# Fused windowed attention and two-layer SiLU network on one core: tile 0's first layer takes a whole batch of 576 tokens, and the zeros of the opening's constants move from GpSimd to VectorE

## The chip, the cores and the metric

The kernel runs on one core of a Trainium2 chip. The metric is the device time of one execution in microseconds (us). All executions quoted here were in the fast state of the chip; their mean granted TensorE clock was 0.988 to 1.000. Engines: PE is TensorE (PEld its weight loads), DVE is VectorE, ACT is ScalarE, POOL is GpSimd, SP is SyncE. All clock times of a trace count from the start of its span, which is some 1.8 us shorter than the device time (301.1 against 302.87 us).

## The reference

Causal attention over a window of 64 positions, then a network of two layers on its output:

```python
B, H, S, D = 8, 8, 576, 64                       # q, k, v: float32
scores = q @ k.T / sqrt(D)                       # kept where 0 <= pos_q - pos_k < 64
attn   = softmax(scores) ; o = attn @ v
x = o.transpose(0, 2, 1, 3).reshape(4608, 512)   # 8 batches x 576 tokens
h = x @ w_in                                     # 512 -> 2048
g = h * sigmoid(h)                               # SiLU
out = g @ w_out                                  # 2048 -> 512, float32
```

## The kernel before

The program is put in order when it is built: each operation joins a queue of its class with a modelled duration, and a list scheduler emits one instruction stream per engine by rank. Four points matter here.

GpSimd issues nearly all loads (these convert float32 to bfloat16 on the way) and also makes the constants. Its stream at the start is four q/k loads, the identity, the window mask, two more q/k loads, four v loads, ten w_in loads, then the rows of batch 1 mixed with eight pieces of w_out.

```python
FIRST, SPLIT, SECOND_LOADS = 6, 12, "0w1w2w3vwvwvwvww"
...
def const_ident(_):
    nc.gpsimd.memset(ident, 0.0)
    nc.gpsimd.affine_select(out=ident, in_=ident, compare_op=ALU.not_equal, fill=1.0, ...)

def const_window(_):
    nc.gpsimd.memset(window, 0.0)
    nc.gpsimd.affine_select(out=window, ...)       # twice
...
def load_w_in(a, lo, hi):
    nc.gpsimd.dma_start(out=w_in_sb[:, 2 * a:2 * a + 2, lo:hi], in_=w_in[256 * a:256 * a + 256, lo:hi]...)
```

PE is kept warm by filler matmuls on `ident` until the exponentials of batch 0 are out:

```python
def warm(op):
    nc.tensor.matmul(banks[op["bank"][0]][:, 0:384], lhsT=ident, rhs=ident..., start=True, stop=True)
p.add_filler(60, "warm", {"PE": 0.26}, warm, [c_ident], gate=lambda: exps[0][-1]["seen"] is None, pool="all")
```

The network works on nine tiles of 512 tokens: first layer (16 output blocks, 4 matmuls each), SiLU into a `g` buffer per block, second layer. Attention comes out in groups of 192 tokens through `bridge`, the transposed attention output that the first layer reads, so tile 0 takes 6 blocks in two parts, and tile 1 takes 12:

```python
work = [(ft, 0, TT) for ft in range(NFT)]                 # TT = 512, NFT = 16
if j == 0:
    work = [(ft, lo, hi) for lo, hi in ((0, 192), (192, TT)) for ft in range(FIRST)] + work[FIRST:]
elif j == 1:
    work = [(ft, lo, hi) for lo, hi in ((0, 256), (256, TT)) for ft in range(SPLIT)] + work[SPLIT:]
```

Tile 0's second layer goes piece by piece through w_out, because w_out is still landing: each of the eight pieces serves eight of its 64 matmuls. The attention of the next batch is interleaved in the second layers.

```python
order = [(m, f, 0, d_model) for m in range(4) for f in range(NFT)]
if j == 0:
    order = [(m, f, 0, d_model) for f in range(NFT) for m in range(4)]
```

The softmax here doesn't subtract the row's maximum and nothing guards it: scores larger than these inputs give would overflow.

Of the kernel before, what the change touches and what calls it, by code (L numbers as in the profile page):

```python
# [9 lines left out]
BF16 = mybir.dt.bfloat16  # L10
# [4 lines left out]
class Plan:  # L15
# [31 lines left out]
    def run(self):  # L47
# [4 lines left out]
        table, left = "exp", self.count  # L52
        pipe, sent = {True: 1.8, False: 0.0}, []
        events, order = [0.0], []
# [68 lines left out]
def kernel(ctx, tc, q, k, v, w_in, w_out, out):  # L123
    nc = tc.nc
# [12 lines left out]
    NN, NNB, NE, NOT, NGT = 8, 8, 12, 4, NFT + 3  # L137
    FIRST, SPLIT, SECOND_LOADS = 6, 12, "0w1w2w3vwvwvwvww"
    FIRST_LOADS = [(x[0], int(x[1])) for x in "q0 k0 q1 k1 q2 q3 k2 k3 v0 v1 v2 v3".split()]
# [11 lines left out]
    ident = keep.tile([128, 128], BF16, name="ident")  # L151
    zero = keep.tile([128, NP], FP32, name="zero")
    spare = keep.tile([128, NP], FP32, name="spare")
    window = keep.tile([128, 64], BF16, name="window")
# [11 lines left out]
    oxs = [keep.tile([128, 3, 2, D], BF16, name=f"ox{i}") for i in range(NOX)]  # L166
    gts = [keep.tile([128, TT], BF16, name=f"g{i}") for i in range(NGT)]
    ots = [keep.tile([128, d_model], FP32, name=f"ot{i}") for i in range(NOT)]
# [7 lines left out]
        {"at": range(4), "pv": range(4, 6), "mp": range(4, 8), "all": range(8)},  # L176
        rank=dict(prime=-8, early=-10, one=-9, first=-9, dma=-1, ld0=-1, st=-2, silu=-3, out=-2, pv=0, s=1, moe=99, warm=200, turn=2,
                  norm=0, inverse=0, bridge=0, exp=1, mask=1, lift=2, block=2, shift=2, cast=4, late=5, clear=9),
        rank0=dict(turn=-6, cast=-6, lift=-5, shift=-4.5, exp=-4, mask=-4, inverse=-3.5, norm=-3, bridge=-3.2),
# [6 lines left out]
    def const_ident(_):  # L186
        nc.gpsimd.memset(ident, 0.0)
        nc.gpsimd.affine_select(out=ident, in_=ident, compare_op=ALU.not_equal, fill=1.0,
                                base=0, channel_multiplier=1, pattern=[[-1, 128]])

    def const_window(_):

        nc.gpsimd.memset(window, 0.0)
        nc.gpsimd.affine_select(out=window, in_=window, compare_op=ALU.is_ge, fill=-32768.0,
                                base=-1, channel_multiplier=1, pattern=[[-1, 64]])
        nc.gpsimd.affine_select(out=window, in_=window, compare_op=ALU.is_ge, fill=-32768.0,
                                base=64, channel_multiplier=-1, pattern=[[1, 64]])
# [17 lines left out]

    c_ident = p.add("one", {"POOL": 1.3}, const_ident)
    c_vv = [p.add("one", {"DVE": 0.25}, lambda _, i=i: clear_vv(i)) for i in range(NV)]
    c_k = [p.add("one", {"DVE": 0.15}, lambda _, i=i: clear_k(i)) for i in range(NK)]
    c_zero = p.add("one", {"DVE": 0.1}, lambda _: nc.vector.memset(zero, 0.0))
    c_window = p.add("one", {"POOL": 0.6}, const_window)  # L220
    c_bias = [p.add("one", {"DVE": 0.9}, const_bias, [c_window])]
# [6 lines left out]
    def load_first_cast(w, u, kk):  # L228
        nc.gpsimd.dma_start(out=natbs[w][:, 0:S], in_=two(u, kk))  # L229
# [106 lines left out]
    def expo(bank, n):  # L336
        nc.scalar.activation(out=es[n % NE], in_=at_six(bank), func=ACTF.Exp, scale=scale)  # L337
# [30 lines left out]
    def first_layer(bank, j, ft, c, lo, hi):  # L368
        nc.tensor.matmul(  # L369
            banks[bank["bank"][0]][:, lo:hi], lhsT=w_in_sb[:, c, ft * 128:(ft + 1) * 128],  # L370
            rhs=bridge[:, (j * TT + lo) // 64:(j * TT + hi) // 64, c], start=(c == 0), stop=(c == NDC - 1),
        )

    def silu(bank, gt, lo, hi):
        nc.scalar.activation(out=gts[gt][:, lo:hi], in_=banks[bank["bank"][0]][:, lo:hi], func=ACTF.Silu)  # L375

# [34 lines left out]
    def add_first_batch():  # L411
        got = {}
        for what, u in FIRST_LOADS:
# [6 lines left out]
            if u == 0:  # L420
                i = n_nat[0] % NN
                n_nat[0] += 1
                ld = p.add("ld0", {"SP": 0.45}, lambda _, i=i, kk=kk: load_first(i, kk), dma=-0.15 if kk == 0 else 0.7)
                ca = p.add("cast", {"ACT": 0.7, "DVE": 0.56}, lambda e, i=i, w=w: cast_first(e, i, w), [ld])
                nat_free[i] = [ca]
            else:
                ca = p.add("early" if (what, u) in FIRST_LOADS[2:6] else "dma", {"POOL": 0.6}, lambda _, w=w, u=u, kk=kk: load_first_cast(w, u, kk), dma=0.8)
            got[what, u] = (w, ca)
# [33 lines left out]
    def add_v_loads(b, parts, busy):  # L462
        v_landed.setdefault(b, []).extend(
            p.add("dma", {"POOL": 1.0}, lambda e, part=part: load_v(e, b, part), busy, dma=1.1, lat=MARGIN * (b > 0)) for part in parts)

    def add_batch_v(b):
        busy = pv_last.get(b - NV, []) + [c_vv[b % NV]]
        if b >= NIV:
            add_v_loads(b, range(NP), busy)
        lv = v_landed[b]  # L470
        for a, z in ([(i, i + 1) for i in range(NP)] if b < NK else [(0, NP)]):
            sh = [p.add("shift", {"DVE": 0.34, "ACT": 0.64} if b == 0 else {"DVE": 0.1 + 0.18 * (z - a)}, lambda e, hf=hf, a=a, z=z: shift_v(e, b, hf, a, z),
                        lv[a:z], b=b) for hf in range(2)]
            for pj in range(a, z):
                v_done[(b, pj // 2)] = v_done.get((b, pj // 2), []) + sh + [lv[pj]]
# [7 lines left out]
    def add_unit(b, g, which, n0):  # L483
# [11 lines left out]
        for i in range(2 * na):  # L495
            ex = p.add("exp" + first, {"ACT": 0.5}, lambda _, i=i: expo(s["bank"][i], 2 * n0 + i), [s], table="exp", b=b)
            s["untils"][i].append(ex)
            exps.setdefault(b, []).append(ex)
            if b:
                ex = p.add("mask", {"DVE": 0.37}, lambda _, i=i: masking(2 * n0 + i, g), [ex, *c_mask], b=b)  # L500
            ready.append(ex)
# [22 lines left out]
    n_ot, free_ot = [0], {}  # L524

    def add_tile(j):
        gt = {}
        for ft in range(NFT):
            gt[ft] = (n_gt[0] % NGT, [])
            n_gt[0] += 1  # L530
        work = [(ft, 0, TT) for ft in range(NFT)]
        if j == 0:
            work = [(ft, lo, hi) for lo, hi in ((0, 192), (192, TT)) for ft in range(FIRST)] + work[FIRST:]
        elif j == 1:
            work = [(ft, lo, hi) for lo, hi in ((0, 256), (256, TT)) for ft in range(SPLIT)] + work[SPLIT:]
        for i, (ft, lo, hi) in enumerate(work):
# [36 lines left out]
        free_gt.update(uses)  # L573

    add_first_batch()
    add_batch_v(0)


    def warm(op):
        nc.tensor.matmul(banks[op["bank"][0]][:, 0:384], lhsT=ident, rhs=ident.unsqueeze(1).to_broadcast([128, 3, 128]),  # L580
                         start=True, stop=True)

    p.add_filler(60, "warm", {"PE": 0.26}, warm, [c_ident], gate=lambda: exps[0][-1]["seen"] is None,
                 pool="all")
# [52 lines left out]
```

## Time and profile before

| | us |
|---|---|
| device time, median of 3 (range) | 302.37 (302.01 to 303.3) |
| span of the profiled execution | 301.1 |
| last landing of w_in / of w_out piece 5 (pieces counted from 0) | 26.25 / 46.30 |
| start of tile 0's second layer / its last matmul's end | 34.15 / 52.86 |
| start of tile 1's second layer | 69.79 |

The prediction below reads most views of this profile. One that it only summarises also belongs here: the timeline of GpSimd before 27 us. Columns: start, length, engine, line, operation, output<-input, how many in a row, and in brackets the idle time before it and what ended that.

```profile
5.93 4.00 POOL L253 DMA_DIRECT2D vv<-in_v_dram  x4
9.89 7.12 POOL L259 DMA_DIRECT2D w_in_sb<-in_moe_w_in_dram  x10
...
26.53 1.20 POOL L239 DMA_DIRECT2D nat<-in_k_dram  x2 [1.01 <-DMA w_in_sb<-in_moe_w_in_dram]
```

The reader sees an engine that does nothing but issue. A v load holds it 1.00 us, a w_in load 0.71 us, a load of rows 0.60 us. From 4.80 to 17 us it has no gap. Then its later issues wait, one by one, for w_in landings: in this trace it never has more than eight loads of its own in flight. The third row load of k waits for the last w_in landing (26.25 us) and comes 0.28 us after it. From there GpSimd issues again without a gap until the w_out piece at 38.48, the one that lands at 46.30.

### The profile page before, as it was taken

What the parts mean: (1) busy time and instruction counts of PE and PEld (TensorE: products, weight loads), DVE (VectorE), ACT (ScalarE), POOL (GpSimd) and SP (SyncE); (2) the same over time, 40 slices, a digit from 0 to 9 for tenths busy, and PEclk for the clock granted to TensorE, in tenths of its full rate; (3) what the DMA queues carried; (4) which work ended last, traced back from release to release, by engine and by line L of the source; (5) the groups of instructions that cost most, each with busy time, mean ns of one, the idle gap of its engine ahead of it and who ended that gap; (6) DMA issues with size and microseconds to landing.
All of it is one profiled execution on the core that took longest, in us unless ns stands there. A gap on an engine that the chain in (4) does not pass through costs nothing.

```text
span 301.1 us, 8386 instructions
## 1 busy us (share of the span) xinstructions
PE 290.4 (96%) x3588; PEld 145.0 (48%) x3588; DVE 138.0 (46%) x330; ACT 173.1 (57%) x319; POOL 118.0 (39%) x177
## 2 busy tenths in 40 slices
PE   4989988999999999999999999999999999999996
PEld 2555444674544454445444544445444544444444
DVE  2591377977885379436950694066005520000000
ACT  4686453786456754774477438663767366226511
POOL 8957986959797989870400000000000000000000
DMA  8999999999999999991580110011101100010012
GB/s 169 166 171 174 158 164 171 225 130 110 188 169 132 108 182 170 164 105 72 65 86 2 51 59 35 3 37 72 37 0 36 73 37 0 35 72 36 0 70 73
DMA packets 82982, 28.64 MB, mean 95 GB/s; under 512 B 72448, under 2 KB 78208, under 8 KB 82944
## 3 DMA queue, kind: packets, MB, share of 16 engines
q0 software_dynamic: 77184, 18.07, 65.0%
q1 hardware_dynamic: 5760, 10.03, 9.3%
q8 instruction: 28, 0.46, 0.7%
q14 instruction: 10, 0.08, 0.1%
HBM read 36.70 MB, written 9.44 MB: 153 GB/s over the span
## 4 chain that ended last, share of the span: by engine, by line
PE 82%; POOL 9%; DMA 6%; issue 1%; DVE 1%; ACT 1%; POOLq 0%; ACTq 0%; DVEq 0%
PE mp L378 39%; PE mp L369 37%; DMA w_in_sb<-in_moe_w_in_dram 3%; PE mp L349 3%; PE at L331 3%; DMA w_out_sb<-in_moe_w_out_dram 3%; POOL vv L253 2%; POOL w_in_sb L259 2%; POOL nat L239 2%; POOL natb L229 1%; POOL w_out_sb L265 1%; ACT g L375 0%; DVE ot L384 0%; PE at L349 0%; DVE qt L246 0%
## 5 line engine op out<-in xcount | busy, mean ns | idle before, releaser
L378 PE MATMUL mp<-w_out_sb,g 128*128 128x512 bf16 (+2 forms) x608 | 130.2, 368 | 1.8 <-DMA w_out_sb<-in_moe_w_out_dram 1.8
L369 PE MATMUL mp<-bridge,w_in_sb 128*128 128x512 bf16 (+3 forms) x648 | 129.0, 355 | 1.7 <-DVE bridge L363 0.7
L375 ACT ACTIVATE g<-mp 128x512 bf16<-128x512 f32 (+3 forms) x162 | 87.6, 550 | 34.1 <-PE mp L369 32.3
L369 PEld LDWEIGHTS <-w_in_sb 128*128 128x128 bf16 x648 | 62.3, 97 | 66.2 <-issue 8.2
L378 PEld LDWEIGHTS <-g 128*128 128x128 bf16 x608 | 56.1, 98 | 63.5 <-issue 2.7
L384 ACT COPY ot<-mp 128x512 f32<-128x512 f32 (+2 forms) x36 | 20.2, 563 | 59.9 <-PE mp L378 46.1
L340 DVE TENSOR_TENSOR e<-e,mask 128x384 bf16<-128x384 bf16 x84 | 25.9, 347 | 50.0 <-ACT e L337 49.5
L337 ACT ACTIVATE e<-at 128x384 bf16<-128x384 f32 x90 | 37.2, 495 | 19.6 <-PE at L331 19.4
L239 POOL DMA_DIRECT2D nat<-in_k_dram x56 | 34.1, 617 | 13.7 <-DMA vv<-in_v_dram 5.8
L253 POOL DMA_DIRECT2D vv<-in_v_dram x32 | 32.2, 1020 | 13.4 <-PE mp L349 13.4
L239 POOL DMA_DIRECT2D nat<-in_q_dram x56 | 35.2, 649 | 2.9 <-DMA w_in_sb<-in_moe_w_in_dram 1.9
L363 DVE STREAM_TRANSPOSE bridge<-ox 128x384 bf16<-128x384 bf16 x48 | 24.8, 552 | 0.0
L246 DVE STREAM_TRANSPOSE qt<-nat 128x576 bf16<-128x576 bf16 x28 | 20.7, 786 | 6.8 <-DMA nat<-in_q_dram 6.8
L246 DVE STREAM_TRANSPOSE kt<-nat 128x576 bf16<-128x576 bf16 x28 | 20.6, 781 | 4.3 <-DMA nat<-in_k_dram 4.3
L359 DVE TENSOR_TENSOR ox<-mp,rc 128x384 bf16<-128x384 f32 x43 | 21.4, 535 | 0.1
L356 DVE RECIPROCAL rc<-mp 128x6 f32<-128x6 f32 x43 | 8.0, 190 | 19.7 <-PE mp L349 19.0
L349 PEld LDWEIGHTS <-e 128*32 128x32 bf16 x1152 | 10.9, 95 | 9.4 <-issue 7.9
L299 DVE COPY vv<-vv 64x576 bf16<-64x576 bf16 (+1 forms) x14 | 7.9, 567 | 13.9 <-DMA vv<-in_v_dram 7.7
L349 PE MATMUL mp<-vv,e 128*32 128x65 bf16 x1032 | 12.2, 194 | 0.0
L337 ACT ACT_TABLE_LOAD x7 | 9.0, 1283 | 5.4 <-PE at L331 5.3
L331 PE MATMUL at<-qt,kt 32*128 32x64 bf16 x1008 | 11.5, 190 | 0.0
L331 PEld LDWEIGHTS <-kt 32*128 32x128 bf16 x1008 | 9.3, 92 | 4.3 <-issue 3.4
(50 smaller groups left out, 79.4 us busy)
## 6 DMA issues: line engine op xcount, KB each, us to landing
out_dram<-ot SPq DMA_DIRECT2D x35, 256.0 KB, 2.4
vv<-in_v_dram POOLq DMA_DIRECT2D x32, 144.0 KB, 5.9
nat<-in_q_dram POOLq DMA_DIRECT2D x56, 72.0 KB, 4.5
nat<-in_k_dram POOLq DMA_DIRECT2D x56, 72.0 KB, 3.9
w_out_sb<-in_moe_w_out_dram POOLq DMA_DIRECT2D x8, 256.0 KB, 6.3
w_in_sb<-in_moe_w_in_dram POOLq DMA_DIRECT2D x6, 256.0 KB, 8.4
w_in_sb<-in_moe_w_in_dram POOLq DMA_DIRECT2D x4, 128.0 KB, 4.9
natb<-in_q_dram POOLq DMA_DIRECT2D x3, 144.0 KB, 4.9
```

Source lines behind the costliest of these rows:

```text
L239: nc.gpsimd.dma_start(out=nats[i][32 * h:32 * h + 32].rearrange("p (m x) -> p m x", m=NB), in_=(q, k)[kk][b, 4 * a + h].rearrange("(m p r) ...
L246: nc.vector.transpose(out=to[:, (2 * a + part) * S:(2 * a + part + 1) * S].rearrange("x (m t r) -> x m r t", t=32, r=2), in_=nats[i].rearr ...
L253: queue[e].dma_start(out=vv[b % NV][:, 2 * g0 + 1:2 * g1 + 1:2, 0:D], in_=v[b].rearrange("h s d -> (h s) d").rearrange("(g p) d -> p g d", ...
L331: nc.tensor.matmul(at_six(op["bank"][h])[:, a, x], lhsT=kt[b % NK][r, at:at + 128], rhs=qt[b % NK][r, at:at + 64], start=(s == a == x == 0 ...
L337: nc.scalar.activation(out=es[n % NE], in_=at_six(bank), func=ACTF.Exp, scale=scale)
L340: nc.vector.tensor_mul(es[n % NE], es[n % NE], mask0 if g == 0 else mask)
L349: nc.tensor.matmul(at_pv(bank)[32 * h:32 * h + 32, x, t], lhsT=e_of(b, a, n, h)[:, x, 32 * t:32 * t + 32], rhs=vv[b % NV][:, (4 * a + h) * ...
L359: nc.vector.tensor_mul(oxs[n % NOX], at_pv(bank)[:, :, :, 0:D], rcs[n % NRC].unsqueeze(3).to_broadcast([128, 3, 2, D]))
L363: nc.vector.transpose(out=bridge[:, n0:n0 + 3, 2 * a:2 * a + 2].rearrange("x t s (u i) -> x t s u i", u=2), in_=oxs[n % NOX].rearrange("p ...
L369: nc.tensor.matmul(banks[bank["bank"][0]][:, lo:hi], lhsT=w_in_sb[:, c, ft * 128:(ft + 1) * 128], rhs=bridge[:, (j * TT + lo) // 64:(j * T ...
L375: nc.scalar.activation(out=gts[gt][:, lo:hi], in_=banks[bank["bank"][0]][:, lo:hi], func=ACTF.Silu)
L378: nc.tensor.matmul(banks[bank["bank"][0]][:, 0:hi - lo], lhsT=gts[gt][:, m * 128:(m + 1) * 128], rhs=w_out_sb[:, f, lo:hi], start=(f == 0) ...
```

## The change

The intent is to use the time before 60 us better. Tile 0's first layer takes all 576 tokens of batch 0 while it waits for w_out anyway, so that tile 1 needs only 448; 64 columns of each SiLU block are then copied to tile 1's buffer. The zeros of the constants go to VectorE, the last two q/k loads are issued before the window mask, and the fillers run on a tile of zeros from the first microsecond. One w_out piece moves back in the load order, and some numbers of the scheduler's model are replaced by measured ones.

```diff
-        pipe, sent = {True: 1.8, False: 0.0}, []
+        pipe, sent = {True: 2.0, False: 0.0}, []
-    FIRST, SPLIT, SECOND_LOADS = 6, 12, "0w1w2w3vwvwvwvww"
+    FIRST, SPLIT, SECOND_LOADS = 8, 14, "0w12ww3vwvwvwvww"
+    blank = keep.tile([128, 128], BF16, name="blank")
-    gts = [keep.tile([128, TT], BF16, name=f"g{i}") for i in range(NGT)]
+    gts = [keep.tile([128, NB * 64], BF16, name=f"g{i}") for i in range(NGT)]
@@ ranks: new classes edge=-8.5 (window mask), dma0=-8.7 (last two q/k loads), rest=3 (copies)
     def const_ident(_):
-        nc.gpsimd.memset(ident, 0.0)
     def const_window(_):
-        nc.gpsimd.memset(window, 0.0)
-    c_ident = p.add("one", {"POOL": 1.3}, const_ident)
+    c_zeros = [p.add("one", {"DVE": 0.1}, lambda _, t=t: nc.vector.memset(t, 0.0)) for t in (blank, ident, window)]
+    c_ident = p.add("one", {"POOL": 0.3}, const_ident, c_zeros)
-    c_window = p.add("one", {"POOL": 0.6}, const_window)
+    c_window = p.add("edge", {"POOL": 0.5}, const_window, c_zeros)
+    def rest_of_first(e, g0, g1):
+        copies[e](out=gts[g1][:, 0:NB * 64 - TT], in_=gts[g0][:, TT:NB * 64])
@@ first_layer and silu: the bank is used from column 0
-                ca = p.add("early" if (what, u) in FIRST_LOADS[2:6] else "dma", ..., dma=0.8)
+                ca = p.add("early" if (what, u) in FIRST_LOADS[2:6] else "dma0", ..., dma=0.74)
@@ v loads of batch 0 1.1 -> 1.0, exponentials 0.5 -> 0.39 + 0.2 latency, ScalarE only for later shifts
         if j == 0:
-            work = [(ft, lo, hi) for lo, hi in ((0, 192), (192, TT)) for ft in range(FIRST)] + work[FIRST:]
+            work = [(ft, lo, hi) for lo, hi in ((0, 192), (192, NB * 64)) for ft in range(FIRST)]
+            work += [(ft, lo, hi) for ft in range(FIRST, NFT) for lo, hi in ((0, 256), (256, NB * 64))]
         elif j == 1:
-            work = [(ft, lo, hi) for lo, hi in ((0, 256), (256, TT)) for ft in range(SPLIT)] + work[SPLIT:]
+            done = NB * 64 - TT
+            work = [(ft, lo, hi) for lo, hi in ((done, 256), (256, TT)) for ft in range(SPLIT)]
+            work += [(ft, done, TT) for ft in range(SPLIT, NFT)]
+            for ft in range(NFT):
+                g0, si = gt_first[0][ft]
+                cp = p.add("rest", {"DVE": 0.12, "ACT": 0.24}, lambda e, ...: rest_of_first(e, g0, g1), ...)
@@ fillers
-        nc.tensor.matmul(banks[...][:, 0:384], lhsT=ident, rhs=ident..., start=True, stop=True)
+        nc.tensor.matmul(banks[...][:, 0:384], lhsT=blank, rhs=blank..., start=True, stop=True)
-    p.add_filler(60, "warm", {"PE": 0.26}, warm, [c_ident], ...)
+    p.add_filler(60, "warm", {"PE": 0.26}, warm, c_zeros, ...)
```

More of the change, by code (lines that the diff above doesn't have):

```diff
@@ L176 @@
         {"at": range(4), "pv": range(4, 6), "mp": range(4, 8), "all": range(8)},
-        rank=dict(prime=-8, early=-10, one=-9, first=-9, dma=-1, ld0=-1, st=-2, silu=-3, out=-2, pv=0, s=1, moe=99, warm=200, turn=2,
-                  norm=0, inverse=0, bridge=0, exp=1, mask=1, lift=2, block=2, shift=2, cast=4, late=5, clear=9),
+        rank=dict(prime=-8, early=-10, one=-9, edge=-8.5, first=-9, dma=-1, ld0=-1, dma0=-8.7, st=-2, silu=-3, out=-2, pv=0, s=1, moe=99, warm=200, turn=2,
+                  norm=0, inverse=0, bridge=0, exp=1, mask=1, lift=2, block=2, shift=2, cast=4, rest=3, late=5, clear=9),
         rank0=dict(turn=-6, cast=-6, lift=-5, shift=-4.5, exp=-4, mask=-4, inverse=-3.5, norm=-3, bridge=-3.2),
@@ L369, in first_layer @@
         nc.tensor.matmul(
-            banks[bank["bank"][0]][:, lo:hi], lhsT=w_in_sb[:, c, ft * 128:(ft + 1) * 128],
+            banks[bank["bank"][0]][:, 0:hi - lo], lhsT=w_in_sb[:, c, ft * 128:(ft + 1) * 128],
             rhs=bridge[:, (j * TT + lo) // 64:(j * TT + hi) // 64, c], start=(c == 0), stop=(c == NDC - 1),
@@ L374, in silu @@
     def silu(bank, gt, lo, hi):
-        nc.scalar.activation(out=gts[gt][:, lo:hi], in_=banks[bank["bank"][0]][:, lo:hi], func=ACTF.Silu)
+        nc.scalar.activation(out=gts[gt][:, lo:hi], in_=banks[bank["bank"][0]][:, 0:hi - lo], func=ACTF.Silu)
+    def rest_of_first(e, g0, g1):
+        copies[e](out=gts[g1][:, 0:NB * 64 - TT], in_=gts[g0][:, TT:NB * 64])
     def second_layer(bank, gt, m, f, lo, hi):
@@ L426, in add_first_batch @@
             else:
-                ca = p.add("early" if (what, u) in FIRST_LOADS[2:6] else "dma", {"POOL": 0.6}, lambda _, w=w, u=u, kk=kk: load_first_cast(w, u, kk), dma=0.8)
+                ca = p.add("early" if (what, u) in FIRST_LOADS[2:6] else "dma0", {"POOL": 0.6}, lambda _, w=w, u=u, kk=kk: load_first_cast(w, u, kk), dma=0.74)
             got[what, u] = (w, ca)
@@ L463, in add_v_loads @@
         v_landed.setdefault(b, []).extend(
-            p.add("dma", {"POOL": 1.0}, lambda e, part=part: load_v(e, b, part), busy, dma=1.1, lat=MARGIN * (b > 0)) for part in parts)
+            p.add("dma", {"POOL": 1.0}, lambda e, part=part: load_v(e, b, part), busy, dma=1.0 if b == 0 else 1.1, lat=MARGIN * (b > 0)) for part in parts)
     def add_batch_v(b):
@@ L471, in add_batch_v @@
         for a, z in ([(i, i + 1) for i in range(NP)] if b < NK else [(0, NP)]):
-            sh = [p.add("shift", {"DVE": 0.34, "ACT": 0.64} if b == 0 else {"DVE": 0.1 + 0.18 * (z - a)}, lambda e, hf=hf, a=a, z=z: shift_v(e, b, hf, a, z),
+            sh = [p.add("shift", {"DVE": 0.34, **({"ACT": 0.64} if a > 1 else {})} if b == 0 else {"DVE": 0.1 + 0.18 * (z - a)}, lambda e, hf=hf, a=a, z=z: shift_v(e, b, hf, a, z),
                         lv[a:z], b=b) for hf in range(2)]
@@ L495, in add_unit @@
         for i in range(2 * na):
-            ex = p.add("exp" + first, {"ACT": 0.5}, lambda _, i=i: expo(s["bank"][i], 2 * n0 + i), [s], table="exp", b=b)
+            ex = p.add("exp" + first, {"ACT": 0.39}, lambda _, i=i: expo(s["bank"][i], 2 * n0 + i), [s], lat=0.2, table="exp", b=b)
             s["untils"][i].append(ex)
@@ L524 @@
     n_ot, free_ot = [0], {}
+    gt_first = []
     def add_tile(j):
         gt = {}
+        gt_first.append(gt)
         for ft in range(NFT):
@@ L532, in add_tile @@
         if j == 0:
-            work = [(ft, lo, hi) for lo, hi in ((0, 192), (192, TT)) for ft in range(FIRST)] + work[FIRST:]
+            work = [(ft, lo, hi) for lo, hi in ((0, 192), (192, NB * 64)) for ft in range(FIRST)]
+            work += [(ft, lo, hi) for ft in range(FIRST, NFT) for lo, hi in ((0, 256), (256, NB * 64))]
         elif j == 1:
-            work = [(ft, lo, hi) for lo, hi in ((0, 256), (256, TT)) for ft in range(SPLIT)] + work[SPLIT:]
+            done = NB * 64 - TT
[3 more added lines that the diff above has]
+                g0, si = gt_first[0][ft]
+                cp = p.add("rest", {"DVE": 0.12, "ACT": 0.24}, lambda e, g0=g0, g1=gt[ft][0]: rest_of_first(e, g0, g1), si + free_gt.get(gt[ft][0], []))
+                gt[ft][1].append(cp)
+                free_gt[g0] = free_gt[g0] + [cp]
         for i, (ft, lo, hi) in enumerate(work):
@@ L579, in warm @@
     def warm(op):
-        nc.tensor.matmul(banks[op["bank"][0]][:, 0:384], lhsT=ident, rhs=ident.unsqueeze(1).to_broadcast([128, 3, 128]),
+        nc.tensor.matmul(banks[op["bank"][0]][:, 0:384], lhsT=blank, rhs=blank.unsqueeze(1).to_broadcast([128, 3, 128]),
                          start=True, stop=True)
-    p.add_filler(60, "warm", {"PE": 0.26}, warm, [c_ident], gate=lambda: exps[0][-1]["seen"] is None,
+    p.add_filler(60, "warm", {"PE": 0.26}, warm, c_zeros, gate=lambda: exps[0][-1]["seen"] is None,
                  pool="all")
```

## The prediction

> **What bounds the kernel now.** I read the page first, for the shares by engine and the slices. The columns of the first line are busy time, share of the span and instructions; each digit of the other two is a fortieth of the span.
>
> ```profile
> PE 290.4 (96%) x3588; PEld 145.0 (48%) x3588; DVE 138.0 (46%) x330; ACT 173.1 (57%) x319; POOL 118.0 (39%) x177
> ...
> PE   4989988999999999999999999999999999999996
> ...
> DMA  8999999999999999991580110011101100010012
> ```
>
> TensorE (PE) is busy 96% of 301.1 us, but only from the ninth slice on is it solid. The DMA row is at 8 to 9 tenths for 18 slices and then falls away: for its first 50 us or so the program also has a stream of loads to bring in.
>
> Then the list of who waited for whom on PE, first 100 us (total, times, longest):
>
> ```profile
> PE at L580 <- POOL ident L188: 4.2, 1, 4.2
> PE mp L378 <- DMA w_out_sb<-in_moe_w_out_dram: 1.8, 3, 0.8
> PE mp L369 <- DVE bridge L363: 0.7, 1, 0.7
> PE mp L369 <- ACT g L375: 0.6, 1, 0.6
> ```
>
> Apart from the 4.2 us before the first filler, PE's named waits are 3.1 us, and after 60 us there is none over 0.3 us: every later tile is PE work back to back (64 first-layer matmuls of 512 columns from 86.51 to 100.49, 218 ns each). So the change can only win before 60 us. The timeline of the opening (start, length, instruction, idle before it and what ended that):
>
> ```profile
> 6.43 0.82 PE L580 MATMUL mp<-ident 128*128 128x384 bf16 x2
> ...
> 7.18 1.17 PE L282 MATMUL mp<-ident,natb 128*64 128x128 bf16 x18
> ...
> 9.67 0.69 PE L282 MATMUL at<-ident,natb 128*64 128x128 bf16 x18
> ...
> 18.70 3.17 PE L369 MATMUL mp<-bridge,w_in_sb 128*128 128x192 bf16 x26
> ...
> 19.40 0.61 ACT L375 ACTIVATE g<-mp 128x192 bf16<-128x192 f32 x2
> ...
> 21.90 0.58 DVE L363 STREAM_TRANSPOSE bridge<-ox 128x384 bf16<-128x384 bf16 x1
> 22.53 11.78 PE L369 MATMUL mp<-bridge,w_in_sb 128*128 128x320 bf16 x62 [0.66 <-DVE bridge L363]
> ```
>
> The real first layer starts at 18.70 us, its first SiLU is out only from 19.40 (a table load of 1.28 us ended at 19.27), and the first six output blocks of 192 tokens are followed by a wait for the last attention output of batch 0 at 22.48. Summing, over successive matmuls, the distance between starts minus columns/2.4 GHz minus 2.6 ns, I get 1.6 us lost between 18.7 and 22.5. The same view for PE alone, later:
>
> ```profile
> 34.15 5.54 PE L378 MATMUL mp<-w_out_sb,g 128*128 128x512 bf16 x24
> 39.62 0.55 PE L331 MATMUL at<-qt,kt 32*128 32x64 bf16 x48
> 40.66 1.89 PE L378 MATMUL mp<-w_out_sb,g 128*128 128x512 bf16 x8 [0.49 <-DMA w_out_sb<-in_moe_w_out_dram]
> 43.02 0.59 PE L378 MATMUL mp<-w_out_sb,g 128*128 128x512 bf16 x2 [0.48 <-DMA w_out_sb<-in_moe_w_out_dram]
> ...
> 46.34 1.02 PE L378 MATMUL mp<-w_out_sb,g 128*128 128x512 bf16 x4 [0.85 <-DMA w_out_sb<-in_moe_w_out_dram]
> ...
> 52.88 0.60 PE L369 MATMUL mp<-bridge,w_in_sb 128*128 128x256 bf16 x4
> ...
> 55.07 1.56 PE L369 MATMUL mp<-bridge,w_in_sb 128*128 128x256 bf16 x11 [0.56 <-ACT g L375]
> ```
>
> The second layer of tile 0 starts at 34.15 and is stopped three times by w_out. After 52.88, tile 1 loses 1.5 us more to banks that wait for ScalarE (0.72 us at 54.24 alone, while its table loads). Last, the chain of waits:
>
> ```profile
> 38.48 7.82 DMA w_out_sb<-in_moe_w_out_dram
> 46.30 0.04 issue
> 46.34 1.02 PE mp L378 x4
> ```
>
> From 9.9 to 46.3 us it runs through GpSimd's issues and landings, not through PE. The landing records give the eight pieces of w_out at 29.19, 32.23, 36.19, 40.61, 42.98, 46.30, 48.19 and 49.54 us, and the w_in halves for output blocks 4 to 7 at 19.22 and 20.48. These landings are the real bound of the opening.
>
> **What the Trainium skill says.** "TensorE: Matmul & The Clock Gate", section "Wait — 56ns, not 53.3ns?", gives warm matmuls a start-to-start of N/2.4 GHz plus about 2.5 ns. The trace agrees: median 216 ns at 512 columns, 136 at 320, 109 at 256, 82 at 192. Cutting a matmul in two therefore costs about 2.6 ns. The same page, "Part 1: The HAM clock gate", says that the array starts at half clock and is released after about 3.4 us of activity. The trace agrees: 18 transposes take 1.17 us at 7.18 and 0.69 at 9.67. "ScalarE: Activation LUTs", "What ACT_TABLE_LOAD costs", has 1283 ns for a load; the trace has 1283. "DMA: Bandwidth & Descriptors", "Anatomy of one DMA", fits 2.0 us plus bytes/436e3 (in us), 2.3 us for the 144 KB loads of q and k. Here the trace differs: the first takes 4.04 us alone with the others behind it, the median is 4.9, and successive ones land 0.70 us apart.
>
> **The change, part by part.**
>
> Zeros by VectorE, fillers from the first microsecond. GpSimd loses two memsets (0.26 and 0.15 us); VectorE gets three small ones. From the order of instructions, GpSimd now issues the last two q/k loads before the window mask, so they leave some 0.9 us earlier and the v loads some 0.4 us earlier (5.93 to about 5.5). But before, the load issued at 4.80 landed at 8.79, just 0.71 after its neighbour: the issue gap had not starved the DMA engines. I give the later landings an advance of 0 to 0.35 us, 0.2 taken. PE runs 15 fillers from about 1.3 us and is warm at about 5. The first transposes wait for a landing at 5.28 anyway, then take 0.7 instead of 1.6; the second pair waits for 6.68, the third for 8.08. First scores come at about 8.9 instead of 10.30, exponentials end at about 16.5 instead of 17.97, and the first layer starts near 17.1, 1.5 us earlier.
>
> How much of that survives? Eight blocks of 192 tokens are 32 x 82.6 ns = 2.64 us. Blocks 0 to 3 (1.3 us) are over well before 20.3; blocks 4 to 7 need the w_in half that landed at 20.48, say 20.3, so this part ends at 21.65. The bridge must then be complete: on VectorE, from the second bridge of the first group (about 17.0) there remain four normalisations at 0.545 and four transposes at 0.558 plus a reciprocal, 4.6 us, so 21.6: a tie, I take 21.8. Then 8 x 4 x 162.6 ns = 5.2 us (384 wide) and 8 x 4 x (109 + 136) = 7.84 us: the second layer starts at 34.85, **0.7 us later** than before, with 576 tokens done instead of 512.
>
> The second layer of tile 0. It does 24 matmuls of 218.6 ns and one scores group (0.57), to 40.7, when w_out piece 3 (40.4 to 40.6) is there: the first wait goes. Piece 4 at 42.8, piece 5 at 46.1 still stop it, as w_out's place in the load order is unchanged from piece 3 on (only piece 1 is moved back, to about 34, needed at 36.6). From piece 5 there remain 24 matmuls, one scores and one values group: 5.25 + 0.57 + 0.58 + 0.14, as before (46.34 to 52.88). End of tile 0: 52.7. So the earlier start is swallowed by the landings; 0.2 us is left.
>
> Tile 1 with 448 tokens. 64 x 16 x 4 = 4096 columns fewer, /2.4 GHz = 1.71 us; 8 more matmuls, 0.02. This stretch has no DMA bound, so **1.69 us** goes straight to the end. Its start stays held by the table load (SiLU not before 54.5), and with 192-wide blocks PE has less to do meanwhile: but by 57.1 I count six blocks, 1.98 us of work, against 19 matmuls, 2.07 us, before: even. Afterwards blocks of 192 take PE 0.330 us and ScalarE 0.331, so ScalarE's gaps may show: +0.15 (estimate).
>
> The 16 copies of 64 columns between g buffers: about 0.1 to 0.24 us each (the plan's own numbers), on ScalarE and VectorE while both have idle time, between 23 and 50 us; ScalarE was idle from 35 to 40. Off the path. Tile 2 on: unchanged.
>
> Sum: -0.2 - 1.69 + 0.15 = -1.74; 302.37 - 1.74 = 300.6, rounded to 300.7.
>
> **The rivals.** First, landings move with the earlier issues and the PE waits vanish too: up to 2 us more, 298.7. For it: at 5 to 12 us latencies are only 4 to 5 us, so the queue is short. Against: from 12.8 us on latencies grow to 10, a backlog that earlier issue doesn't shorten. Second, ScalarE or VectorE becomes the bound: the bridge comes at 22.5 as before, or copies queue ahead of exponentials and masks (one copy waits for the last uses of a g buffer, in order), or 192-wide SiLUs pace PE: 0.5 to 1.5 us lost, 301.2 to 302.2. For it: 0.331 against 0.330. Against: ScalarE catches up in the values groups. Third, the gain is only moved: tile 1, shorter, meets the bridge of batch 1 before it is ready. Against: those bridges end at 59.3 before, and the second half of tile 1 would start at about 60.2; close.
>
> **Range and chances.** Two-sided: 299.8 (landings gain) to 302.0 (a new wait eats most). Even the best case is under 2% (296.3 would be needed), and nothing points to a loss of 6 us: faster 0.01, same 0.985, slower 0.005.
>
> **What would show it.** Right: w_out waits of PE near 1.5 us with the last ending at 46.0 to 46.3; second layer of tile 0 from about 34.8; tile 1's first layer from about 52.7 and its end 1.5 to 1.9 us before the old 69.37; transposes at 5.3 in 0.7 us; every later tile shifted by the same amount. Wrong: w_out piece 5 landing a microsecond earlier or later, a PE wait for the bridge near 21.6 or 60, or ScalarE named as the releaser through the 192-wide blocks.

## The result, and the profile after

The changed kernel took **299.77 us** (median of 4, 298.97 to 300.29); the kernel before, run in the same rounds, 302.84 (median of 4). The ratio is 0.9897, 95% interval 0.9858 to 0.9936. Here and below a ratio is the one on record, from fast runs of the same rounds, so it is not quite the ratio of the medians quoted; gains in us are differences of means. The result is correct. The prediction was 300.7 with a range from 299.8; the gain is about 3.1 us where 1.7 were expected.

Shares and slices of the kernel after, from the page, read as those of before:

```profile
PE 289.6 (97%) x3641; PEld 149.1 (50%) x3641; DVE 138.2 (46%) x340; ACT 176.3 (59%) x340; POOL 117.8 (40%) x175
...
PE   7979999899999999999999999999999999999996
...
DMA  8999999999999999992950210011001100110012
```

The share of PE rose by one point and says little. The DMA row falls away at the same place, the nineteenth slice, as before.

The four longest waits of PE in the first 100 us of the kernel after (total, times, longest):

```profile
PE mp L369 <- DMA w_in_sb<-in_moe_w_in_dram: 1.5, 1, 1.5
PE at L595 <- DVE blank L215: 1.0, 1, 1.0
PE mp L282 <- DMA natb<-in_q_dram: 0.9, 1, 0.9
PE mp L369 <- ACT g L375: 0.8, 1, 0.8
```

The first line is as predicted (w_in until 20.23 us). The second is the start, 3.2 us earlier than the old 4.2, and the third the first q load, which landed at 6.06 us against 5.28 before; the last is tile 1's start behind the table load, as before. What is missing is the surprise: no wait for w_out is in the list, where before had 1.8 us. PE's timeline of the kernel after, around the end of tile 0:

```profile
34.48 5.17 PE L381 MATMUL mp<-w_out_sb,g 128*128 128x512 bf16 x23
...
40.06 3.21 PE L381 MATMUL mp<-w_out_sb,g 128*128 128x512 bf16 x13
...
51.12 0.82 PE L369 MATMUL mp<-bridge,w_in_sb 128*128 128x192 bf16 x8
...
53.24 1.73 PE L369 MATMUL mp<-bridge,w_in_sb 128*128 128x192 bf16 x16 [0.82 <-ACT g L375]
```

The second layer starts at 34.48, later than before as predicted, but runs on to 51.09 instead of 52.86. In the control run below that has no wait for w_out (`nat_delay`), the same stretch takes 16.36 us, from 34.01 to 50.37; here it takes 16.61. So the landings now hold only some 0.25 us in it: one gap of 0.24 us before piece 4, too short for the list. The chain of waits of the kernel after shows where those remain:

```profile
15.66 9.28 DMA w_in_sb<-in_moe_w_in_dram
...
25.22 3.58 POOL nat L239 x6
...
35.68 6.53 DMA w_out_sb<-in_moe_w_out_dram
...
42.25 1.02 PE mp L381 x4
```

The chain has the same links as before: the w_in issues of GpSimd, the last w_in landing, GpSimd's issues from 25.22 on, a landing of w_out. It ends one piece earlier, with piece 4. Piece 5, at 44.49, lands just before PE comes to it: of the nine matmuls from 43.69 the first four belong to piece 4, and the first of piece 5 starts at 44.56. GpSimd's timeline of the kernel after, beside the one of before:

```profile
5.44 4.01 POOL L253 DMA_DIRECT2D vv<-in_v_dram  x4
9.37 6.99 POOL L259 DMA_DIRECT2D w_in_sb<-in_moe_w_in_dram  x10
...
25.22 1.19 POOL L239 DMA_DIRECT2D nat<-in_k_dram  x2 [0.84 <-DMA w_in_sb<-in_moe_w_in_dram]
```

The v loads are issued 0.49 us earlier (predicted: about 0.4), the first w_in load 0.52 and the last 0.65 us earlier; but the last w_in landing, and with it the third row load of k, is **1.31 us** earlier. In this pair, loads issued 0.5 to 0.65 us earlier landed about twice that much earlier. The third profile of the kernel after (in the table below) warns against a rule: its last w_in issue, at 16.35, is no earlier than the old 16.31, and yet it landed at 25.53.

Every profiled execution of before and after, with repeats from later rounds (us):

| | before | before, repeat | after | after, repeat | after, third |
|---|---|---|---|---|---|
| last w_in landing | 26.25 | 26.33 | 24.94 | 25.11 | 25.53 |
| landing of w_out piece 5 | 46.30 | 45.77 | 44.49 | 44.33 | 45.14 |
| end of tile 0 | 52.86 | 52.40 | 51.09 | 50.90 | 51.76 |
| end of tile 0 to tile 1's second layer | 16.93 | 16.93 | 15.41 | 15.41 | 15.41 |
| from there to the end of the span | 231.3 | 231.4 | 231.1 | 231.1 | 231.1 |

Tile 1 gives 1.52 us, every time. The end of tile 0 gives 1.77 us in the first pair; by the means of the columns, (52.86 + 52.40)/2 less (51.09 + 50.90 + 51.76)/3, it gives 1.38. The rest gives 0.2. That is 3.1 us by means, as the device times say. The landings of one and the same program scatter by some 0.8 us, so a single profile can't tell a few tenths.

### The profile page after: what moved, and what is told of

Same layout as the page of the kernel before. It is cut to its first block, busy times and chain, and to the rows that moved or that the text cites. A ratio compares the mean times of both kernels' runs of the same rounds, so it can differ in the third digit from the quotient of the medians.

```text
span 297.6 us, 8516 instructions
## 1 busy us (share of the span) xinstructions
PE 289.6 (97%) x3641; PEld 149.1 (50%) x3641; DVE 138.2 (46%) x340; ACT 176.3 (59%) x340; POOL 117.8 (40%) x175
## 4 chain that ended last, share of the span: by engine, by line
PE 84%; POOL 8%; DMA 5%; issue 1%; ACT 1%; POOLq 0%; ACTq 0%
PE mp L381 40%; PE mp L369 37%; PE at L331 3%; DMA w_in_sb<-in_moe_w_in_dram 3%; PE mp L349 3%; DMA w_out_sb<-in_moe_w_out_dram 2%; POOL w_in_sb L259 2%; POOL nat L239 2%; POOL vv L253 2%; POOL natb L229 1%; POOL w_out_sb L265 1%; ACT ot L387 0%; ACT g L375 0%; PE at L349 0%; POOL window L193 0%
## 5 line engine op out<-in xcount | busy, mean ns | idle before, releaser
L369 PE MATMUL mp<-bridge,w_in_sb 128*128 128x512 bf16 (+5 forms) x696 | 128.6, 342 | 3.1 <-DMA w_in_sb<-in_moe_w_in_dram 1.5
L375 ACT ACTIVATE g<-mp 128x512 bf16<-128x512 f32 (+5 forms) x174 | 89.6, 523 | 32.0 <-PE mp L369 30.8
L369 PEld LDWEIGHTS <-w_in_sb 128*128 128x128 bf16 x696 | 66.2, 97 | 63.6 <-issue 7.3
L239 POOL DMA_DIRECT2D nat<-in_k_dram x56 | 35.0, 643 | 10.6 <-DMA nat<-in_q_dram 3.4
L363 DVE STREAM_TRANSPOSE bridge<-ox 128x384 bf16<-128x384 bf16 x48 | 24.7, 551 | 0.0
```

Source lines behind the costliest of these rows:

```text
L239: nc.gpsimd.dma_start(out=nats[i][32 * h:32 * h + 32].rearrange("p (m x) -> p m x", m=NB), in_=(q, k)[kk][b, 4 * a + h].rearrange("(m p r) ...
L363: nc.vector.transpose(out=bridge[:, n0:n0 + 3, 2 * a:2 * a + 2].rearrange("x t s (u i) -> x t s u i", u=2), in_=oxs[n % NOX].rearrange("p ...
L369: nc.tensor.matmul(banks[bank["bank"][0]][:, 0:hi - lo], lhsT=w_in_sb[:, c, ft * 128:(ft + 1) * 128], rhs=bridge[:, (j * TT + lo) // 64:(j ...
L375: nc.scalar.activation(out=gts[gt][:, lo:hi], in_=banks[bank["bank"][0]][:, 0:hi - lo], func=ACTF.Silu)
```

## The experiments

The open question is why w_out came so much sooner. **The tile theory**: wider tiles and the new plan shift what GpSimd issues and what it collides with, and the opening as such gives 0.2 us as predicted. **The issue theory**: GpSimd's time before its last w_in issue is on the path that sets the end, one for one or more, through the landings of w_in and w_out. **The load order**: the moved w_out piece. Besides there are the early fillers, which keep PE warm but touch no load. Each text on record says in its own words which of these it weighs. All 16 kernels gave correct results. The kernel before was run in the same rounds throughout (means 302.5, 302.7, 303.1 and 302.9 us in the four sets of rounds).

### Opening only

The changed kernel with tile 0 back at 512 tokens.

```diff
-    FIRST, SPLIT, SECOND_LOADS = 8, 14, "0w12ww3vwvwvwvww"
+    FIRST, SPLIT, SECOND_LOADS = 6, 12, "0w12ww3vwvwvwvww"
@@ tile 0 and tile 1: work lists as before, no copies
```

> The changed kernel with tile 0 at 512 tokens again (six blocks, then twelve, as before); zeros by VectorE, early fillers, GpSimd's order of issues and the moved loads stay. Theory (the landings come earlier because GpSimd issues v and w_in some 0.5 us earlier): w_out piece 5 lands near 44.5 us as in the changed kernel, tile 0's second layer ends 1.3 to 1.8 us earlier than 52.9, and the time is 1.2 to 1.8 us under before (ratio 0.994 to 0.996). Rival (the landings only differ from execution to execution, and the tokens are the whole gain): piece 5 near 46.3, ratio 0.998 to 1.001.

Measured: 301.63 us, ratio 0.9973 [0.9942, 1.0004], a gain of 0.9 us. In its profile piece 5 landed at 45.30 and tile 0 ended at 51.86, 1.0 us before the old 52.86. This lies between its two expectations, and the interval just includes no gain. By its profile the opening alone earns something through the landings, if less than in company; PE also waited 1.0 us there for VectorE's transposes of k (near 39 us), which the changed kernel doesn't.

### Tokens only

The kernel before with the 576/448 split and the copies, nothing of the opening.

```diff
-    FIRST, SPLIT, SECOND_LOADS = 6, 12, "0w1w2w3vwvwvwvww"
+    FIRST, SPLIT, SECOND_LOADS = 8, 14, "0w1w2w3vwvwvwvww"
@@ g buffers, work lists and copies as in the change
```

> The kernel before with only tile 0 at 576 tokens and tile 1 at 448 (eight and fourteen blocks, copies between g buffers). Theory: w_out piece 5 lands near 46.3 us as before, tile 0's second layer ends near 52.9, tile 1's first layer is 1.7 us shorter, ratio 0.9945. Rival (tokens are the whole gain): ratio 0.990.

Measured: 300.80 us, ratio 0.9949 [0.9919, 0.9978], a gain of 1.6 us. This is nearly the whole of what was predicted for the change (1.74). It leaves about 1.5 us of the 3.1 to the opening, where the prediction had 0.2.

What was expected of its landings missed. In its profile the w_in issues began at 9.84, as before, and yet the last w_in landing came at 25.36, piece 5 at 44.94 and the end of tile 0 at 51.68, which is 0.7 to 1.2 us earlier than in the two profiles of the kernel before. This execution was the fastest of its six (300.54, mean 300.93), and two PE stalls of 0.3 us later on took back a part; by the mean times the tokens earn little more than the 1.52 us of tile 1. But landings can come early without the opening, so the tile theory is not excluded for a part of the gain.

### Constants back on GpSimd

The changed kernel with the memsets of `ident` and `window` on GpSimd and the window mask ahead of the last two q/k loads; the early fillers stay.

```diff
+        nc.gpsimd.memset(ident, 0.0)
+        nc.gpsimd.memset(window, 0.0)
-    c_zeros = [... for t in (blank, ident, window)]
+    c_zeros = [... for t in (blank,)]
-    c_ident = p.add("one", {"POOL": 0.3}, const_ident, c_zeros)
+    c_ident = p.add("one", {"POOL": 1.3}, const_ident)
-    c_window = p.add("edge", {"POOL": 0.5}, const_window, c_zeros)
+    c_window = p.add("one", {"POOL": 0.6}, const_window)
```

> The changed kernel, but ident and window are zeroed by GpSimd again and the window mask again stands ahead of the last two k loads; early fillers and 576 tokens stay. Theory (GpSimd's issue times set the landings): piece 5 lands near 46 us again, the time loses 1.2 to 1.8 us of the 3.1, ratio 0.994 to 0.996. Rival (PE's earlier and warmer start does it): piece 5 stays near 44.5, ratio 0.990.

Measured: 300.98 us, ratio 0.9953 [0.9919, 0.9986], a gain of 1.55. Nearly all of the opening's gain is gone, with the fillers still early. Its first w_in issue is back at 9.84 us, its last w_in landing at 26.46, piece 5 at 45.79. So half a microsecond of GpSimd's time seems worth some 1.5 us at the end, though with intervals of about 1 us on both gains, from different rounds, the factor is uncertain. That speaks for the issue theory: scores start at 9.02 in its profile, as in the changed kernel (9.00), so the start of PE is not what was lost.

### Late fillers

The changed kernel with the fillers tied to the identity in the plan, as before.

```diff
-    p.add_filler(60, "warm", {"PE": 0.26}, warm, c_zeros, ...
+    p.add_filler(60, "warm", {"PE": 0.26}, warm, [c_ident], ...
```

> The changed kernel, but the fillers wait for the identity as before, so PE starts at about 4 us and is cold in the first transposes; all else stays. Theory: the landings don't depend on PE; piece 5 near 44.5, ratio 0.990 to 0.991. Rival (the warm clock is what lets the opening run ahead): the first layer starts 1 us later and the end of tile 0 moves with it, ratio 0.993 to 0.995.

Measured: 300.78 us, ratio 0.9944 [0.9912, 0.9976], a gain of 1.7: this too lost some 1.4 us of the gain, though its w_in issues begin at 9.37 as in the changed kernel. That is the ratio that its rival had named, a warm PE that lets the opening run ahead. The edit did less than was meant: a filler reads only `blank`, so five of them still ran from 0.99 us, where the changed kernel has 15. Then PE stood idle for 1.6 us, and 18 transposes at 7.05 took 1.17 us instead of 0.69. In this profile the first scores came at 10.09 us and the first layer started at 17.93 (16.24 to 16.85 in the changed kernel), and PE had waits of 1.3 us for the bridge and 1.6 us for w_out. That execution was the slowest of its six (301.59), with piece 5 at 46.28, so it can't show the typical case. The two parts of the opening don't add up: each taken away alone costs nearly all that both earn. What the early fillers earn by themselves stays open.

### GpSimd idle time ahead of the v loads

To measure the issue theory without any other change: the changed kernel plus six memsets (1.5 us in all) of a tile that nobody reads, after the window mask. The order of instructions on every other engine is the same.

```diff
+    waste = keep.tile([128, 128], BF16, name="waste")
@@ const_window, at its end
+        for _ in range(6):
+            nc.gpsimd.memset(waste, 0.0)
```

> The changed kernel with six idle memsets of 128x128 on GpSimd (about 1.5 us by the 0.26 us of one in the trace of before) between the window mask and the first v load; the order on every other engine is the same. Theory (issue-bound landings): the w_in and w_out landings and the end of tile 0 come 1.2 to 1.6 us later, ratio rises by 0.004 to 0.005 against the unaltered one of this call. Rival (the backlog behind w_in absorbs it): w_in pieces late by under 0.5 us, ratio as the unaltered.

Measured: 302.71 us, ratio 0.9994 [0.9971, 1.0018]; the changed kernel in the same rounds (next) has 0.9895. So 1.5 us of GpSimd's time cost **3.0 us**, all that the change earns. Last w_in landing 28.00, piece 5 47.95, end of tile 0 54.55. Two repeats and one undone part went with it:

The changed kernel again, unedited:

> The changed kernel, unaltered, for a second profile and more timed runs. If the 3.1 us were right: ratio 0.989 to 0.991 and w_out piece 5 near 44.5 us. If the first four runs were a lucky draw: ratio 0.992 to 0.994, piece 5 anywhere between 44.5 and 46.3.

Measured: 299.59 us, ratio 0.9895 [0.9877, 0.9914].

The kernel before again, as a kernel to be tested:

> The kernel before, unaltered, for a second profile: how far do landings scatter between executions of one and the same program? Theory (issue times set the landings): piece 5 within 0.3 us of 46.30 again. Rival (scatter): a difference of 1 us or more. Ratio 1.000 within 0.3%.

Measured: 302.88 us, ratio 1.0006 [0.999, 1.0022]. Its profile has the old late landing of w_in, 26.33, so that was no accident of the first profile; though its last w_in issue was at 16.95 instead of 16.31.

The changed kernel with the old load order:

```diff
-    FIRST, SPLIT, SECOND_LOADS = 8, 14, "0w12ww3vwvwvwvww"
+    FIRST, SPLIT, SECOND_LOADS = 8, 14, "0w1w2w3vwvwvwvww"
```

> The changed kernel with the old order of the second batch's loads (w_out piece 1 before the third group of rows). Both theories: nothing from piece 3 on moves, and piece 1 is needed only at 36.6, so ratio as the unaltered one within 0.2%. If it loses 0.5 us or more, the moved loads carry a part of the gain.

Measured: 299.45 us, ratio 0.9893 [0.9875, 0.9911], piece 5 at 44.47. The load order does nothing that these runs can tell: that rival falls.

### GpSimd idle time ahead of w_in only

The same six memsets, now after the last v load, so that scores, values and bridges of batch 0 are not held up.

```diff
@@ load_w_in, at its start
+        if a == lo == 0:
+            for _ in range(6):
+                nc.gpsimd.memset(waste, 0.0)
```

> The changed kernel with the same six idle memsets (1.5 us) on GpSimd, now between the last v load and the first w_in load; all other engines have the same order. Theory (every us that GpSimd loses up to the last w_in issue goes to w_out piece 5, and then to the end): piece 5 at 46 us or later, ratio 0.994 to 0.999, against 0.9895 of the unaltered. Rival (only the early v loads, and with them the attention, matter): piece 5 within 0.5 us of 44.4, ratio 0.990.

Measured: 302.71 us, ratio 0.9982 [0.9962, 1.0003]: a loss of 2.6 us against the ratio 0.9897 of the changed kernel, which is from other rounds, and of 2.9 against the next kernel, of the same rounds. The attention of batch 0 was not touched (last bridge at 21.04, against 20.75 to 21.3 in the changed kernel). Waits of PE in its first 100 us:

```profile
PE mp L373 <- DMA w_in_sb<-in_moe_w_in_dram: 2.4, 2, 1.5
PE mp L385 <- DMA w_out_sb<-in_moe_w_out_dram: 1.1, 2, 0.7
```

The two lines name most of the cost, 2.0 us: 2.4 us for w_in instead of 1.5, and 1.1 us for w_out, where the list of the changed kernel has none. The first scores are no part of it. Four of these six runs, and three of the six with the earlier pause, had a mean granted clock of 0.989 to 0.994; without all runs below 0.999 the losses are still 2.8 and 2.6 us, so a slower clock is not the reason.

### GpSimd idle time after the last w_in issue

The control: the same six memsets one instruction group later.

```diff
@@ load_w_in, at its end
+        if a == 1 and hi == d_ff:
+            for _ in range(6):
+                nc.gpsimd.memset(waste, 0.0)
```

> The changed kernel with the six idle memsets after the last w_in issue (about 16.4 us), where GpSimd soon stands still anyway until loads land. Theory (there it is held by landings, so 1.5 us of its time are free): piece 5 within 0.4 us of 44.4, ratio 0.989 to 0.991. Rival (any time that GpSimd loses costs the end): ratio 0.994 or more.

Measured: 299.17 us (298.61 to 301.49), ratio 0.9885 [0.9855, 0.9915]: no loss. The same idle work costs 2.6 to 2.9 us ahead of w_in and nothing behind it, because there GpSimd waits for w_in landings anyway. Together the two runs settle the place: it is GpSimd's time up to its last w_in issue that costs the kernel when it grows.

### w_out ahead of v in the load order

If landings bound tile 0, w_out might come first: the changed kernel with another order, and the same with one w_in load cut in two.

```diff
-    FIRST, SPLIT, SECOND_LOADS = 8, 14, "0w12ww3vwvwvwvww"
+    FIRST, SPLIT, SECOND_LOADS = 8, 14, "0w12ww3wvwwvvwvw"
@@ in the second kernel, besides
-    for lo, hi in ((0, 256), (256, 512), (512, 1024), (1024, 1536), (1536, 2048)):
+    for lo, hi in ((0, 256), (256, 512), (512, 768), (768, 1024), (1024, 1536), (1536, 2048)):
```

> The changed kernel with w_out pieces 3 to 6 moved ahead of one v load each or so (order after the fourth rows: w v w w v v w v w). Theory (tile 0's end is piece 5's landing plus 6.6 us): piece 5 about 1 us earlier than 44.4, PE then reaches it without a wait; PE itself gets there only at 44.5, so 0 to 0.5 us under the unaltered, ratio 0.988 to 0.9895. Rival (the later v loads become the wait): ratio 0.991 or more.

Measured: 302.71 us, ratio 1.0003 [0.9973, 1.0033]: all the gain lost, although piece 5 landed at 42.33 and tile 0 ended at 50.71. The later v loads made the build-time plan move attention of batch 1 behind tile 0, where PE waits three times (0.52 us for ScalarE, 1.25 and 0.48 us for VectorE); and then, by stretches of 4 us of its profile (start:end, length, busy time and instructions of PE, PEld, DVE, ACT and POOL, granted PE clock, DMA share, GB/s; the DMA share can pass 1, because a packet's whole time is counted where it starts):

```profile
52.00:56.00 4.00, 2.17 (x67) 1.77 (x61) 4.00 (x13) 1.14 (x3) 4.00 (x6) 0.93 1.28 289
56.00:60.00 4.00, 4.00 (x34) 3.77 (x33) 4.00 (x8) 2.45 (x8) 3.77 (x6) 0.64 2.14 164
```

PE's clock was granted 0.93 and then 0.64 of full speed; the 192-wide matmuls of tile 1 started 160 ns apart between 55.45 and 58.7, instead of 82. From the end of tile 0 to tile 1's second layer it took 18.47 us instead of 15.41; the slow matmuls are some 1.6 us of that (21 x 78 ns). A short series of gaps in PE's work, and in this execution the slow clock after it, cost more than w_out gave. The clock is not all of it: two of the six runs (302.36 and 304.67) had a mean clock of 1.000 and were no faster.

> w_first with the w_in load of blocks 4 to 7 cut in two (blocks 4 and 5 land first), aimed at PE's wait of 0.9 to 1.5 us for w_in near 19 us. Theory: that wait shrinks by about 0.6 us and the end by 0.3 to 0.7 us, ratio 0.986 to 0.988. Rival: two more issues of 0.7 us on GpSimd push all later landings by that much, and nothing is won, ratio 0.990 or more.

Measured: 304.04 us, ratio 1.0034 [1.001, 1.0058], slower than before. The w_in wait of PE was gone, but two more issues on GpSimd put the last w_in landing at 26.51 and piece 5 at 44.14; tile 0 ended at 52.17. The gaps behind tile 0 and the slow clock came here too (17.93 us to tile 1's second layer), and the rest took 1.1 us more than in the changed kernel.

### How large is the cost, and can it be turned round?

The last set asks whether the cost is one for one or two for one, and repeats the control. First the changed kernel a third time:

> The changed kernel, unaltered, as the control of this call: ratio 0.989 to 0.9905, w_out piece 5 near 44.4 us.

Measured: 300.18 us (299.91 to 300.36), ratio 0.9911 [0.9896, 0.9926], a gain of 2.7 us, a little less than expected; piece 5 at 45.14.

Two memsets (0.5 us) instead of six ahead of w_in:

> The changed kernel with two idle memsets (0.5 us) between the last v load and the first w_in load. Theory (GpSimd's lost time counts about double): 0.9 to 1.2 us over the control of this call. Rival (one for one): 0.4 to 0.6 us. Second rival (the backlog absorbs small delays, only large ones count): 0 to 0.2 us.

Measured: 300.59 us, ratio 0.9938 [0.9913, 0.9962], mean 300.83 against 300.16 for the changed kernel in the same rounds: 0.67 us for 0.5 to 0.6 us, about one for one by the means. But its six runs lie between 299.99 and 302.01 us (the slowest with a mean clock of 0.994; 0.43 us without it), so they settle neither one for one nor two for one.

The control once more, unedited from above:

> The pause of 1.5 us behind the w_in issues once more. Theory (issuing disturbs the moving w_in packets): 0.4 to 0.8 us under the control of this call, last w_in landing at 24.3 to 24.7 us. Rival (scatter): within 0.2 us of the control.

Measured: 299.67 us (299.21 to 300.03), ratio 0.9894 [0.9878, 0.991].

Twelve memsets after the last w_in issue:

> The pause doubled to 3.1 us, to about 19.5 us, where GpSimd would else be held by landings for most of the time. Theory: as nat_delay, last w_in at 24.3 to 24.7, time within 0.3 us of it. Rival (the rows of batch 1 now come late): 1 us or more over the control.

Measured: 299.36 us (299.14 to 299.84), ratio 0.9887 [0.9871, 0.9902]. GpSimd's timeline of this kernel has the pause and what follows it:

```profile
17.05 3.10 POOL L266 MEMSET waste<- 128x128 bf16 x12
20.18 2.45 POOL L240 DMA_DIRECT2D nat<-in_q_dram  x4
```

Even 3.1 us without any issue cost nothing: the row loads start at 20.18 instead of 16.36. By means of the same rounds this kernel is 0.7 us and the shorter pause 0.5 us faster than the changed kernel, so it is the fastest of its rounds; but the intervals of the ratios overlap, four runs each, and I don't call that gain shown. What was expected of the landings missed: the last w_in landing came at 25.21 and 25.19 in the two profiles with the pause, not at 24.3 to 24.7.

## Why the prediction was right or wrong

- **Tile 1, 448 tokens: right.** 1.69 less 0.15 was predicted, 1.54; measured 1.52 in three profiles. SiLU pacing and the bridge of batch 1 cost no more than was allowed: the list shows ACT g with 0.8 us in all, and no bridge wait near 60.
- **Opening of PE and the tie of the bridge: right in kind.** Scores came at 9.00 (8.9 predicted; 10.30 before), w_in held PE until 20.23 (20.3). The first layer started at 16.24 to 16.85 (17.1), and the bridge was ready at 20.75 to 21.3, not 21.6 to 21.8, so the second layer started at 34.12 to 34.48, not 34.85. In the first profile 0.25 us of this went to a landing (piece 4).
- **Landings: this step failed.** The prediction says: "I give the later landings an advance of 0 to 0.35 us, 0.2 taken", because "the issue gap had not starved the DMA engines". Pieces 3, 4 and 5 came at 39.58, 42.21 and 44.49, that is 1.0, 0.8 and 1.8 us earlier; by the means of two and three profiles piece 5 came 1.4 us earlier. The text drew the chain through GpSimd's issues from 9.9 us on and then judged the issues by one landing gap at 8.79, at the start of the v loads. GpSimd's issue time before w_in was on that very chain: 1.5 us added there cost 2.6 to 3.0 us, the same after it nothing.
- **How much of the 1.4 us this explains is not settled.** In the six traces whose w_in issues begin at 9.37 to 9.45 without an added pause (the changed kernel three times, opening only, late fillers, old load order), the last w_in landing has a mean of 25.3 and piece 5 of 45.0; in the four that begin at 9.84 to 9.89 (two of before, tokens only, constants back), 26.1 and 45.7. So 0.5 us of issue time goes with landings 0.7 to 0.8 us earlier, whichever the tiles. The single groups overlap (25.4 to 26.5 against 24.9 to 25.8 for w_in). For the remainder the early start of PE is a rival that no run has taken apart, and the late fillers lost about as much as the late issues.
- **Two slips in the reading.** The DMA row's 18 full slices are 135 us (a slice is 7.5 us), not "its first 50 us or so"; the reading has no part in the sum. The 2.3 us for a load of q or k is an estimate from the page's fit and the converted size.
- **The sum.** With 1.4 in place of 0.2 for the end of tile 0, and 1.52 for tile 1, the prediction's own sum is 2.9 of the 3.1 us. The last 0.2 us, after the start of tile 1's second layer, was predicted as zero and not studied; both profiles of before have one PE stall of 0.28 us there (at 191.80 and 191.38), the three of after none.
- **The first rival**, "landings move with the earlier issues and the PE waits vanish too", came nearly true. Its counter-argument, a backlog that earlier issue doesn't shorten, was the wrong one.

Why longer delays cost more than one for one **stays open**. By 24 us the changed kernel had moved 213 KB more than the one before (103 KB in the second pair of profiles), so DMA engines did carry more in the same time. In the kernel before, 45 of the 1024-byte packets before 26 us, nearly all of them of w_in, took over 200 ns (usual: 98 ns). All these packets together took 16.4 us over the usual; spread over 16 engines, the 9.1 us that the changed kernel has less would be 0.57 us. Over the first 14 traces, 5.6% of such packets were slow while GpSimd was issuing a w_in load, and 0.8% while it was idle (4.8% and 0.8% over all 18). But the repeat of before had 12 slow packets and landed as late. This is a correlation, and no run took that cause away by itself.

## What to carry to other kernels

Where one engine issues the loads and the chain of waits runs through those issues, its instruction time ahead of the last issue can be kernel time, as 1.5 us was here: take constants and other small work off it, or move them behind that issue. Ask of each idle stretch whether a wait behind it is for a landing (then work there is free) or for an issue. A reordering that feeds the bound sooner can still lose by the gaps that it opens on PE.

## What the Trainium skill lacked or had wrong

- "DMA: Bandwidth & Descriptors", section "Anatomy of one DMA", calls descriptor generation "small, variable" and does not count it there as time of the engine that issues (further down the page calls the time to initiate a DMA "usually small relative to the DMA itself"); "Perfetto Trace Analysis", section What "DMA-bound" means, does name an issuing engine solid with DMA slices as one of the bounds, and this trace agrees (GpSimd without a gap from 9.37 to 16.36 us). What both lack is how long one load holds the engine. Here GpSimd was held 0.56 us by a q/k load, 0.70 by a w_in load, 1.02 by a v load and 0.60 by a load of rows, and 1.5 us of its time ahead of w_in cost 2.6 to 3.0 us of the kernel.
- "TensorE: Matmul & The Clock Gate", section "HAM oscillation — how this bites in real kernels", gives the rule "no PE-idle gaps >~3.4µs". In the kernel with w_out first, the largest distance between starts of successive matmuls from 50.3 to 55.4 us was 1.45 us (others 0.89 and 0.73), and yet the granted clock was 0.64 from 56 to 60 us: several shorter gaps in a row were followed by a slower clock. The page's next section does describe frequent short idles that throttle. It is no rule either way: the kernel before had distances of 0.68, 0.86 and 1.23 us between 39.9 and 46.4 us and kept a clock of 1.
- None of the pages that I read has the slow packets: 1024-byte packets of w_in that took over 200 ns (usual 98), 5.6% of them while GpSimd was issuing a w_in load against 0.8% while idle, in 14 traces. Their cause is open.
